# The last wo rows of every layer on 128 partitions, in one transfer over all 16 DMA engines

## The chip, the cores and the metric

The kernel runs on one core of one Trainium2 chip. The metric is the device time of one execution in microseconds (us), here about 1998 us. A single run of the kernel before scatters with a standard deviation of about 1.0 us, one of the changed kernel with about 0.7 us.

## The reference

Four layers of decode attention for one token: A, B, A, B. All arrays are bf16; x has 640 values, there are 32 heads of 192 values, and the caches hold 8192 positions.

```python
x = x + attn(layernorm(x), k_cache, v_cache, wq, wo)      # four times, with the arrays of A, B, A, B

def attn(x, k_cache, v_cache, wq, wo):
    q = (x @ wq).reshape(32 heads, 192)
    p = softmax(q . k_cache * 192 ** -0.5)                # over 8192 positions
    return (p . v_cache).reshape(6144) @ wo               # wo: 6144 x 640
```

Nearly all of the work is reading: the profile counts 848 MB from HBM.

## The kernel before

All loads go through one queue, issued by SyncE. Eight memory slots of 3 MB hold K blocks, V blocks and weights in turn; a transfer is issued when its slot is free. VectorE multiplies K by q in place, TensorE (PE) sums the products, the softmax follows, and PE multiplies by V.

The output projection of a layer is done in four pieces: three blocks of 10 heads (`wo`, 1920 rows each) and a *tail*, `wol`, the 384 rows of the last two heads. The change touches the tail alone. Before, in layers 0 to 2, it lay on 64 partitions with 6 rows each; in layer 3 on 128 partitions with 3 rows each.

```python
O_PART = [P // 2, P // 2, P // 2, P]                      # P = 128
OI = [O_LAST * DH // n for n in O_PART]                   # rows on a partition: 6, 6, 6, 3
# ...
def transfer(n):
    # ...
    if n[0] == "wol":
        r0 = o["wol"] * DH
        if O_PART[l] == P:                                # 128 partitions, one transfer
            return SP.op(lambda s: s.dma_start(
                wol_rows(l), w["wo"][r0:r0 + O_LAST * DH].rearrange("(p i) n -> p (i n)", p=P)),
                *free, sem=semOL, inc=16)
        k = O_PART[l] // O_LAST                           # 64 partitions: one transfer of 32 for each head
        for h in range(O_LAST):
            e = SP.op(lambda s, h=h: s.dma_start(
                wol_rows(l)[h * k:(h + 1) * k],
                w["wo"][r0 + h * DH:r0 + (h + 1) * DH].rearrange("(q e i) n -> e q (i n)", e=8, i=OI[l])),
                *free, sem=semOL, inc=16)
        return e
# ...
def values(h):                                            # the last two heads are written in the tail's order
    # ...
    q = 1 if O_PART[l] == P else O_PART[l] // O_LAST // 8
    parts = [(o_sb[...].rearrange("p (i e q) -> p q e i", i=OI[l], q=q), OB[par][...]) for i in range(2)]
# ...
def gather_last(h):                                       # transposes a head's output: k = OI[l] columns
    n, k = O_PART[l] // O_LAST, OI[l]
    for c in range(k):
        for i in range(2):
            PE.op(lambda t, c=c, i=i: t.matmul(TB[r0:r0 + n, c:c + 1], lhsT=o_sb[...], rhs=pick[:, i:i + 1], ...))
# ...
def project(n, rows, o, ev_o):                            # OI[l] * 5 matmuls for the tail
    for i in range(k):
        for c in range(DC):
            PE.op(lambda t, i=i, c=c: t.matmul(YB[:, c:c + 1], lhsT=t3[:, i, c:D:DC], rhs=o[:, i:i + 1], ...))
```

The source pattern of the old form, `(q e i) n -> e q (i n)` with `e=8`, looks odd.

## Time and profile before

| | before |
|---|---|
| median of the first three runs | 1998.22 us (1997.81 to 1998.73) |
| span of the profiled run | 1996.3 us |
| DMA, main queue, share of 16 engines | 99.3% |
| PE / VectorE busy | 70% / 52% |
| instruction fetches (packets of queue q8) | 71 |

The page of the whole execution. The GB/s line has 40 slices of 50 us; part 3 lists each DMA queue with its packets, megabytes and share of the 16 engines.

```profile
span 1996.3 us, 20649 instructions
PE 1397.3 (70%) x10555; PEld 321.0 (16%) x7611; DVE 1047.7 (52%) x1074; ACT 220.3 (11%) x665; POOL 4.5 (0%) x22
GB/s 412 429 432 428 431 430 429 431 430 430 429 431 429 430 430 430 429 430 430 429 379 430 430 431 428 432 429 430 431 429 426 431 428 431 430 430 430 429 430 335
q1 hardware_dynamic: 40064, 848.38, 99.3%
q8 instruction: 71, 1.16, 0.2%
```

DMA is the bound. The queue runs at about 430 GB/s in all slices but the first, the last and the 21st, the boundary of layers 1 and 2 (379). One packet of 24,576 bytes takes 914 ns in the packet records, 26.9 bytes/ns for one engine.

The boundary of layers 1 and 2, PE's instructions in order of time (start us, duration us, what; in brackets the idle time before and what ended it):

```profile
1017.31 3.16 PE L465 MATMUL YB<-oT,pool 128*128 128x1 bf16 x75 [1.13 <-DMA pool<-in_B_wo_dram]
1020.40 1.35 PE L465 MATMUL YB<-oTl,pool 64*128 64x1 bf16 x30
1022.28 0.59 PE L373 MATMUL TB<-small,ones 128*128 128x2 f32 x2 [0.52 <-DVE small L371]
1023.39 1.78 PE L407 MATMUL QM<-wq,xb 128*128 128x384 bf16 x5 [0.52 <-DVE xb L386]
```

PE waits for the third wo block, projects it (75 matmuls), projects the tail (30 matmuls, 1.35 us), and the next layer starts. The DMA queue runs dry in this stretch (the lowest slice of a window view from 985 to 1050 us is 88 GB/s, just after 1019 us; the spread of a transfer's 16 landings falls from 11.06 us, from 1011.9 us on, to 2.12 us, from 1029.3 us on), so a microsecond here is a microsecond of the kernel.

The end of the chain of waits (start us, duration us, what), and PE's last instructions:

```profile
1932.77 6.77 DVE pool L495 x4
...
1940.07 6.78 DVE pool L495 x4
...
1948.74 43.57 DMA pool<-in_B_wo_dram
1992.32 0.05 issue
1992.36 0.77 PE YB L465 x15
```
```profile
1991.54 0.74 PE L465 MATMUL YB<-oTl,pool 128*128 128x1 bf16 x15
1992.36 0.76 PE L465 MATMUL YB<-oT,pool 128*128 128x1 bf16 x15
```

**Lags of the engines.** In the semaphore records of the trace the transfers of 128 partitions leave 16 landings each, and the six tail transfers of layers 0 to 2 leave 8 each. I take a landing for the end of one engine's share. Sorted, they show how far the engines are apart. An engine keeps its lag from one transfer to the next (the 16 sorted lags at 1406.6 us and at 1413.9 us agree within 0.01 us), so it can be followed. At the third wo block of layer 2 (landed 1507.31 to 1511.72 us) the lags behind the first engine were, in us, H being the half that carries the tail and U the other (which engine belongs to which half shows from the tail's own 16 landings, eight engines twice, 1.15 to 1.17 us apart):

```
H: 0.00 0.00 0.16 0.75 1.81 2.09 3.23 4.21
U: 0.03 0.23 3.06 3.19 3.24 3.25 3.31 4.41
```

Engines fall behind in steps, most of about 1.5 us, just after a 16,384-byte packet of queue q8 (behind the one at 1737.83 us, for example, the largest lag goes from 8.14 to 9.69 us). The profile calls that queue "instruction". There are 71 such packets beside PE's 10,555 matmuls and 7,611 weight loads, one for 255.9 PE instructions. I call such a packet a *fetch*.

### The profile page before, as it was taken

What the parts mean: (1) busy time and instruction counts of PE and PEld (TensorE: products, weight loads), DVE (VectorE), ACT (ScalarE), POOL (GpSimd) and SP (SyncE); (2) the same over time, 40 slices, a digit from 0 to 9 for tenths busy, and PEclk for the clock granted to TensorE, in tenths of its full rate; (3) what the DMA queues carried; (4) which work ended last, traced back from release to release, by engine and by line L of the source; (5) the groups of instructions that cost most, each with busy time, mean ns of one, the idle gap of its engine ahead of it and who ended that gap; (6) DMA issues with size and microseconds to landing.
All of it is one profiled execution on the core that took longest, in us unless ns stands there. A gap on an engine that the chain in (4) does not pass through costs nothing.

```text
span 1996.3 us, 20649 instructions
## 1 busy us (share of the span) xinstructions
PE 1397.3 (70%) x10555; PEld 321.0 (16%) x7611; DVE 1047.7 (52%) x1074; ACT 220.3 (11%) x665; POOL 4.5 (0%) x22
## 2 busy tenths in 40 slices
PE   4667767667576766666777676776776768767776
PEld 1111112111311211211041111121112212111112
DVE  3554554556255456455725545545663455654563
ACT  0111111111011111111011111111101111111111
POOL 0000000000000000000000000000000000000000
PEclk9888877889678788888977878888887788887888
DMA  9999999999999999999999999999999999999997
GB/s 412 429 432 428 431 430 429 431 430 430 429 431 429 430 430 430 429 430 430 429 379 430 430 431 428 432 429 430 431 429 426 431 428 431 430 430 430 429 430 335
DMA packets 40296, 849.69 MB, mean 426 GB/s; under 512 B 4688, under 2 KB 4688, under 8 KB 5136
## 3 DMA queue, kind: packets, MB, share of 16 engines
q1 hardware_dynamic: 40064, 848.38, 99.3%
q8 instruction: 71, 1.16, 0.2%
q14 instruction: 17, 0.14, 0.0%
q10 hardware_dynamic: 144, 0.00, 0.0%
HBM read 848.36 MB, written 0.00 MB: 425 GB/s over the span
## 4 chain that ended last, share of the span: by engine, by line
DMA 69%; PE 18%; DVE 11%; ACT 1%; issue 1%; another core or an unknown queue 0%; SPq 0%; DVEq 0%
DMA pool<-in_B_k_cache_dram 32%; DMA pool<-in_A_k_cache_dram 30%; PE S L58 12%; DVE pool L495 9%; DMA pool<-in_B_wo_dram 4%; PE O L546 2%; DMA pool<-in_A_wo_dram 2%; DMA x_bf<-in_A_x_dram 1%; PE S L508 1%; PE TB L569 1%; PE QT L427 1%; DVE s_sb L516 1%; PE YB L465 1%; ACT p_sb L526 1%; PE TB L530 0%
## 5 line engine op out<-in xcount | busy, mean ns | idle before, releaser
L495 DVE TENSOR_TENSOR pool<-pool,q_sb 128x3072 bf16<-128x3072 bf16 x512 | 865.7, 1754 | 398.8 <-DMA pool<-in_A_k_cache_dram 204.7
L58 PE MATMUL S<-pool,ident 128*128 128x512 bf16 x2944 | 803.4, 427 | 34.6 <-DVE pool L495 34.5
L546 PE MATMUL O<-pool,p_sb 128*2 128x384 bf16 x4096 | 340.1, 414 | 0.0
L508 PE MATMUL S<-pool,ident 128*128 128x512 bf16 x128 | 61.3, 479 | 223.9 <-DVE pool L495 223.9
L516 DVE TENSOR_REDUCE s_sb<-S 128x64 f32<-128x512 f32 x128 | 88.4, 690 | 237.0 <-PE S L58 237.0
L569 PE MATMUL TB<-o_sb,small 128*1 128x192 f32 x480 | 123.9, 391 | 38.1 <-DVE small L534 27.1
L546 PEld LDWEIGHTS O<-pool,p_sb 128*2 128x2 bf16 x4096 | 128.1, 87 | 128.1 <-issue 91.8
L453 ACT ACTIVATE q_sb<-QM 128x192 bf16<-128x192 f32 x120 | 39.6, 330 | 964.1 <-PE QM L446 964.1
L446 PEld LDWEIGHTS QM<-ident,qT 128*128 128x128 bf16 x240 | 23.2, 98 | 745.3 <-issue 729.8
L530 PE MATMUL TB<-small,ones 128*128 128x1 f32 x256 | 50.3, 266 | 109.9 <-ACT p_sb L526 109.9
L520 PE MATMUL QM<-ident,m_bf 128*128 128x128 bf16 x128 | 27.8, 217 | 122.9 <-DVE m_bf L519 121.2
L561 ACT ACTIVATE o_sb<-O,small 128x384 f32<-128x384 f32 (+1 forms) x136 | 77.2, 579 | 224.5 <-PE O L546 224.5
L534 DVE RECIPROCAL small<-TB 128x1 f32<-128x1 f32 x128 | 21.6, 168 | 122.9 <-PE TB L530 122.9
L526 ACT ACTIVATE p_sb<-s_sb,small 128x64 bf16<-128x64 f32 x128 | 44.5, 348 | 268.5 <-DVE small L523 268.5
L523 DVE TENSOR_REDUCE small<-QM 128x1 f32<-128x128 f32 x128 | 37.3, 292 | 63.3 <-PE QM L520 63.3
L575 ACT ACTIVATE orow<-TB 1x192 bf16<-1x192 f32 x120 | 38.3, 319 | 202.7 <-PE TB L569 202.7
L530 PEld LDWEIGHTS TB<-small,ones 128*128 128x128 f32 x256 | 39.5, 194 | 130.4 <-ACT p_sb L526 130.4
L508 PEld LDWEIGHTS S<-pool,ident 128*128 128x128 bf16 x128 | 12.8, 100 | 283.6 <-DVE pool L495 283.3
L520 PEld LDWEIGHTS QM<-ident,m_bf 128*128 128x128 bf16 x128 | 12.3, 96 | 216.7 <-ACT q_sb L453 126.9
L569 PEld LDWEIGHTS TB<-o_sb,small 128*1 128x1 f32 x480 | 33.5, 89 | 81.4 <-DVE small L534 36.0
L465 PE MATMUL YB<-oT,pool 128*128 128x1 bf16 x900 | 38.1, 178 | 6.6 <-DMA pool<-in_A_wo_dram 3.2
L465 PEld LDWEIGHTS YB<-oT,pool 128*128 128x128 bf16 x900 | 37.0, 131 | 7.6 <-DMA pool<-in_A_wo_dram 3.4
(50 smaller groups left out, 220.0 us busy)
## 6 DMA issues: line engine op xcount, KB each, us to landing
pool<-in_B_k_cache_dram SPq DMA_DIRECT2D x64, 3072.0 KB, 35.5
pool<-in_A_k_cache_dram SPq DMA_DIRECT2D x63, 3072.0 KB, 27.7
pool<-in_A_v_cache_dram SPq DMA_DIRECT2D x63, 3072.0 KB, 33.5
pool<-in_B_v_cache_dram SPq DMA_DIRECT2D x60, 3072.0 KB, 37.0
pool<-in_A_wo_dram SPq DMA_DIRECT2D x6, 2400.0 KB, 25.8
pool<-in_B_wo_dram SPq DMA_DIRECT2D x5, 2400.0 KB, 33.9
pool<-in_A_wq_dram SPq DMA_DIRECT2D x1, 7680.0 KB, 20.9
pool<-in_B_wq_dram SPq DMA_DIRECT2D x1, 7680.0 KB, 29.5
```

The source lines that it names most:

```text
L58: return t.add_instruction(mybir.InstMatmult(name=t.bass.get_next_instruction_name(), engine=mybir.EngineType.PE, ins=[t.lower_ap(rhs), t. ...
L453: lambda a: a.activation(q_sb[i][:], QM[:, 0:DH], ACT.Copy), e, last["q"][i], bank=use["QM"])
L465: e = PE.op(lambda t, i=i, c=c, f=y_first[0], fin=end and i == k - 1: t.matmul(YB[:, c:c + 1], lhsT=t3[:, i, c:D:DC], rhs=o[:, i:i + 1], s ...
L495: e = DV.op(lambda v, d0=d0: v.tensor_tensor(k3[:, :, d0:d0 + QD], kin[:, :, d0:d0 + QD], q_sb[qi][:, d0:d0 + QD].unsqueeze(1).broadcast_t ...
L508: t.matmul(S[:, :], lhsT=ident[:], rhs=k3[:, :, d0:d0 + R], start=True, stop=fin) if d0 == 0 else
L516: ev_s = DV.op(lambda v: v.tensor_reduce(s_sb[par][:], S[:].rearrange("p (j r) -> p j r", r=R), AX.X, ALU.add), ev_S[h], last["s"][par], b ...
L520: e = PE.op(lambda t: t.matmul(QM[:, C_MX:C_MX + P], lhsT=m_bf[par][:, 0:1].broadcast_to([P, P]), rhs=ident[:], start=True, stop=True), ev ...
L526: ev_p[h] = AC.op(lambda a: a.activation(p_sb[pi][:], s_sb[par][:], ACT.Exp, bias=negm[par][:, 0:1], accum_out=l_col[par][:]), ev_n, ev_s, ...
L530: e = PE.op(lambda t: t.matmul(TB[:, C_L + par:C_L + par + 1], lhsT=ones[:, 0:1].broadcast_to([P, P]), rhs=l_col[par][:], start=True, stop ...
L546: e = PE.op(lambda e, g=g, j=j, f=m < G, fin=fin: e.matmul(OB[par][32 * g:32 * g + 2, 0:2 * DH], lhsT=p_sb[pi][:, j:j + 2], rhs=t[:, j * D ...
L561: ev_os[h] = AC.op(lambda a, o=o, i=i: a.activation(o, i, ACT.Copy, scale=rl[pi][:, 0:1]), e, ev_rl[h], last["osb"], bank=use[f"O{par}"])
L569: e = PE.op(lambda t, i=i: t.matmul(TB[0:1, C_O:C_O + DH], lhsT=pick[:, i:i + 1], rhs=o_sb[:, i * DH:(i + 1) * DH], start=(i == 0), stop=( ...
```

## The change

The intent is that all 16 engines share the tail of every layer, as they did in layer 3 already (16 landings there). Everything else follows from `O_PART`: one transfer instead of two, 3 rows on a partition instead of 6, 15 projection matmuls instead of 30, and half of the transposes.

```diff
-    O_PART = [P // 2, P // 2, P // 2, P]
+    O_PART = [P] * NL
```

## The prediction

> **What bounds the kernel now.** DMA. The page of the whole execution gives the main queue 99.3% of the 16 engines' span at 425 GB/s; PE is busy 70%, DVE 52%. The chain of waits is 69% DMA. A 24,576-byte packet takes 914 ns: 26.9 B/ns an engine. The slices drop only at the layer 1 to 2 boundary (379 GB/s) and at the end.
>
> **The change.** In layers 0 to 2 the last 384 rows of wo (480 KB) arrive as two transfers of 32 partitions, source dimension 8 outermost. [...] these six transfers leave 9 semaphore updates each (8 landings and one write by the queue), all others 16. So half the engines get 8 packets of 7,680 B (291 ns each, 2.33 us) and the other half nothing. After it every engine gets 8 packets of 3,840 B (149 ns, measured in layer 3, which has this form already): 1.19 us. Bytes stay equal. Also, per layer, 15 fewer projection matmuls (30 take 1.35 us in the timeline, so -0.65 us), 24 fewer transposing matmuls, each with its weight load: 78 PE instructions less, 234 in all.
>
> **What lies on the critical path.** Not the mean of the engines but the last one. From the 16 landing times of each transfer I followed the engines' lags. They grow by about 1.5 us whenever an instruction fetch (16 KB, queue q8, 71 of them) falls on an engine; they reset at the layer 1 to 2 boundary, where the queue runs dry.
> - Layer 0: the latest engine is one of the untouched half (lag 5.0 us, against 3.5 in the half that takes the load). Evening out gains nothing; the untouched half loses 1.19 us.
> - Layer 1 to 2 boundary: the third wo block's last landing (1017.3 us) starts the projection. The loaded half lags 8.8, the other 8.0; with layer 0 evened out they become about 7.6 and 9.2: +0.4 us. The shorter projection then gives -0.65 us, on the chain. Net about -0.2 us.
> - Layer 2: the latest engine is in the loaded half (4.2 before, 6.5 after). It stays latest to the end: lag 11.2 at the last landing (1992.3 us). It gains 1.14 us; the worst of the other half rises from 8.0 to 9.2.
> - The last fetch (at 1989.4 us) falls on that same latest engine and costs 1.5 us. With 234 PE instructions less it should come past the end or not at all; then the other half's 9.2 is the end: -2.0 us instead of -1.1.
>
> Sum: -0.2 and -1.1 to -2.0; I take -1.9.
>
> **Predicted: 1996.3 us, 1994.5 to 1998.8 eight times in ten. Faster by over 2%: 0.003; within 2%: 0.994; slower: 0.003.**
>
> **What would show it.** The queue's packets: 192 of 7,680 B gone, 384 more of 3,840 B. wo's tail transfers with 16 landings within the spread of the engines. The DMA share unchanged at 99%; 70 or 71 fetches; projection of the tail 15 matmuls in 0.7 us; span near 1994.4 us. The last landing near 1990.4.
>
> **What would make it wrong.** Fetches falling on other engines: each costs 1.5 us on one, and the latest one decides. If they fall on the half that now carries more, the gain vanishes or turns into +1 us. A gain of several us would mean that the DMA idled at boundaries where I read none.

The sum: -0.2 us at the boundary and -1.1 to -2.0 at the end, together -1.3 to -2.2, of which -1.9 was taken. That 234 PE instructions are about one fetch is an estimate from the trace of before (255.9 PE instructions to a fetch).

## More of the kernel before

The chain says that the kernel ends 0.8 us after the last DMA landing (1992.32). But PE had been busy with the tail's projection until 1992.28 (1991.54 + 0.74). It waited for the DMA for less than 0.1 us.

## The result, and the profile after

| | before | after |
|---|---|---|
| median, first comparison | 1998.01 us (4 runs) | 1996.58 us (4 runs, 1996.25 to 1997.43) |
| ratio | | 0.9994, 95% interval 0.9977 to 1.0011 |
| span of the profiled run | 1996.3 | 1994.7 |
| last landing before the output | 1992.32 | 1990.08 |
| instruction fetches | 71 | 70 |

A ratio is the mean time of one kernel's fast runs over that of the other's of the same rounds, so it isn't quite the ratio of the medians. The changed kernel was compared three times, on three occasions; the differences of the means were -1.21, -0.89 and -1.49 us. Taken together (14 runs against 22) that is -1.23 us with a standard error of 0.29: a real gain of 0.06%.

The page after:

```profile
span 1994.7 us, 20412 instructions
PE 1392.6 (70%) x10438; PEld 318.0 (16%) x7494; DVE 1047.4 (53%) x1074; ACT 220.3 (11%) x665; POOL 4.5 (0%) x22
GB/s 410 431 431 428 432 429 429 430 431 430 428 430 431 428 432 428 431 429 429 431 382 431 428 431 428 431 430 429 431 429 427 430 430 429 430 429 429 429 432 345
q1 hardware_dynamic: 40256, 848.38, 99.4%
q8 instruction: 70, 1.15, 0.2%
```

The bytes are equal, there are 192 packets more, 117 matmuls and 117 weight loads fewer (234 PE instructions), and one fetch fewer. The boundary of layers 1 and 2:

```profile
1017.86 3.16 PE L465 MATMUL YB<-oT,pool 128*128 128x1 bf16 x75 [0.51 <-DMA pool<-in_B_wo_dram]
1020.88 0.74 PE L465 MATMUL YB<-oTl,pool 128*128 128x1 bf16 x15
1022.14 0.59 PE L373 MATMUL TB<-small,ones 128*128 128x2 f32 x2 [0.52 <-DVE small L371]
1023.25 1.78 PE L407 MATMUL QM<-wq,xb 128*128 128x384 bf16 x5 [0.52 <-DVE xb L386]
```

PE starts on the third wo block 0.55 us *later* (+0.4 predicted), the tail's projection is 0.61 us shorter (-0.65 predicted), and the next layer's q starts 0.14 us earlier (-0.2 predicted). In the two later traces of the changed kernel q starts at 1023.26 and 1023.45, that is 0.13 us earlier and 0.06 us later than before; the sum is thus no larger than its scatter. The end:

```profile
1937.39 1.61 another core or an unknown queue
1939.02 6.77 DVE pool L495 x4
...
1981.81 1.37 another core or an unknown queue
1983.22 2.76 PE O L546 x32
...
1987.86 3.71 PE YB L465 x90
1991.59 0.16 DVE x_bf L633
```
```profile
1990.21 0.74 PE L465 MATMUL YB<-oTl,pool 128*128 128x1 bf16 x15
1990.81 0.74 PE L465 MATMUL YB<-oT,pool 128*128 128x1 bf16 x15
```

"Another core or an unknown queue" is the profile's name for a release that it could not attribute; by the landing records the first was a K block (landed 1939.0), the second the last V block (landed 1983.18). The last landing (1990.08) has left the chain. PE multiplies by the last V block from 1983.22 on, and the final 90 matmuls run without a stop from 1987.86 on; what the end now follows from is that V block and the compute behind it. In the three traces of this kernel the last landing was at 1990.08, 1990.28 and 1990.22, but the span 1994.7, 1996.4 and 1995.3.

### The profile page after: what moved, and what is told of

The parts are those of the page before. It is cut to its first block, busy times and chain, and to the rows that moved or that the text cites. A ratio compares the mean times of both kernels' runs of the same rounds, so it can differ in the third digit from the quotient of the medians.

```text
span 1994.7 us, 20412 instructions
## 1 busy us (share of the span) xinstructions
PE 1392.6 (70%) x10438; PEld 318.0 (16%) x7494; DVE 1047.4 (53%) x1074; ACT 220.3 (11%) x665; POOL 4.5 (0%) x22
## 3 DMA queue, kind: packets, MB, share of 16 engines
q1 hardware_dynamic: 40256, 848.38, 99.4%
## 4 chain that ended last, share of the span: by engine, by line
DMA 65%; PE 21%; DVE 12%; ACT 1%; issue 1%; another core or an unknown queue 0%; DVEq 0%
DMA pool<-in_B_k_cache_dram 32%; DMA pool<-in_A_k_cache_dram 30%; PE S L58 13%; DVE pool L495 10%; PE O L546 3%; DMA pool<-in_B_wo_dram 2%; PE TB L569 1%; DMA x_bf<-in_A_x_dram 1%; PE S L508 1%; PE YB L465 1%; DVE s_sb L516 1%; ACT p_sb L526 1%; PE QT L427 1%; PE TB L530 1%; DVE small L523 0%
## 5 line engine op out<-in xcount | busy, mean ns | idle before, releaser
L546 PE MATMUL O<-pool,p_sb 128*2 128x384 bf16 x4096 | 346.5, 420 | 1.4 <-DMA pool<-in_B_v_cache_dram 1.4
L520 PEld LDWEIGHTS QM<-ident,m_bf 128*128 128x128 bf16 x128 | 12.3, 96 | 215.3 <-ACT q_sb L453 126.9
```

Source lines behind the costliest of these rows:

```text
L520: e = PE.op(lambda t: t.matmul(QM[:, C_MX:C_MX + P], lhsT=m_bf[par][:, 0:1].broadcast_to([P, P]), rhs=ident[:], start=True, stop=True), ev ...
L546: e = PE.op(lambda e, g=g, j=j, f=m < G, fin=fin: e.matmul(OB[par][32 * g:32 * g + 2, 0:2 * DH], lhsT=p_sb[pi][:, j:j + 2], rhs=t[:, j * D ...
```

## The experiments

Twelve runs were made, two of them of the changed kernel as it is. "Before" and "after" are the two kernels above. The theory at the outset: the latest DMA engine counts, not the mean of the 16; fetches and the shorter projection do the rest. Rivals: the balance alone, the instructions alone, or chance.

### The changed kernel again: e0_after_again and g_after_third

No edit. Expected of the first:

> The changed kernel once more, for the size of chance. Theory (the last DMA engine's lag decides): span of the profile within 0.7 us of 1994.7, 70 instruction fetches, landings of the final transfer spread over 7.5 to 9 us, because the fetches fall on the same engines in the same order. Rival (the 1.4 us between the kernels are chance): the span differs by more than 1 us, and the ratio to the kernel before lies on either side of 1.

Measured: 1996.74 us (median of 5), ratio 0.9995 (0.9983 to 1.0008), 70 fetches, last landings spread over 7.95 us. The span of the profiled run was 1996.4, not within 0.7 us of 1994.7: that part of the expectation failed, though the last landing repeated within 0.2 us. By that mark the rival, chance, did better: the spans differ by 1.7 us, though the ratio lies on the same side of 1 as in the first comparison (0.9994). Only the three comparisons together (-1.23 us, standard error 0.29) speak against chance. The end of its chain hangs on a K block (landed 1939.27), and from its multiplication on there is compute alone:

```profile
1939.29 6.78 DVE pool L495 x4
...
1989.17 3.71 PE YB L465 x90
```

This was the first sign that the end is not decided by the last landing.

> The changed kernel a third time, as the base of the two doses on the same chip. Theory: about 1 us under before, 70 fetches; the last landing 1.5 to 2.2 us earlier than in the first trace of before, but the end of the span set by the compute chain of the last heads, not by the last landing.

Measured: 1997.17 us, ratio 0.9992 (0.9979 to 1.0004), 70 fetches, last landing 1990.22 (2.1 us earlier than in the trace of before), span 1995.3. The end of its chain:

```profile
1939.94 47.92 DMA pool<-in_B_wo_dram
1987.86 0.05 issue
1987.91 3.77 PE YB L465 x90
```

It waits for the third wo block (last landing 1987.86), which is followed by the tail and by a last piece of that block; then all 90 matmuls run through, and the last landing at 1990.22 falls within them. The gain, the fetches and the earlier last landing came as expected, and the last landing doesn't set the end. But what sets it here is not the compute chain either: PE waited for a transfer, the third wo block, whose last landing came 2.4 us before the very last. That part of the expectation failed.

### Either half of the change alone: e1_spread_only and e2_short_only

First the balance without the fewer instructions: 64 partitions stay, but in one transfer, meant for 16 engines.

```diff
-                if O_PART[l] == P:
+                if True:
                     return SP.op(lambda s: s.dma_start(
-                        wol_rows(l), w["wo"][r0:r0 + O_LAST * DH].rearrange("(p i) n -> p (i n)", p=P)),
+                        wol_rows(l), w["wo"][r0:r0 + O_LAST * DH].rearrange("(p i) n -> p (i n)", p=O_PART[l])),
@@ values
-                    q = 1 if O_PART[l] == P else O_PART[l] // O_LAST // 8
+                    q = 1
```

> Tail of wo over 16 engines in layers 0 to 2, but still on 64 partitions: 4 packets of 7,680 B on every engine, the same PE instructions as before (71 fetches). Theory: the layer 1 to 2 boundary is not helped (0 to +0.4 us), the latest engine of the end gains 1.16 us and keeps the last fetch: last landing near 1991.4, time 0.7 to 1.1 us under before. Rival 1 (the gain is the shorter projection and fewer instructions): 0. Rival 2 (the gain is the balance alone): the whole 1.4 to 2 us of the change.

Then the fewer instructions without the balance: 128 partitions, in two transfers in the old pattern with `e=8`, which left 8 landings each in before.

```diff
-                if O_PART[l] == P:
+                if l + 1 == NL:
@@ values
-                    q = 1 if O_PART[l] == P else O_PART[l] // O_LAST // 8
+                    q = 1 if l + 1 == NL else O_PART[l] // O_LAST // 8
```

> Tail of wo on 128 partitions (234 PE instructions fewer), but still on 8 engines: 16 packets of 3,840 B (2.38 us)[...]. Theory: the projection at the boundary gives -0.65 us and the last fetch (number 71) goes, which had put 1.54 us on the latest engine: spread of the last landings 9.7 instead of 11.2, time about 2 us under before, so as good as the full change, though the engines are as uneven as before. Rival 1 (shorter projection only, no fetch): -0.65 us with 71 fetches. Rival 2 (balance): 0.

Measured: both kernels were *slower* than either of the whole ones: 2005.91 us (ratio 1.0045, 1.0032 to 1.0057) and 2007.30 us (1.0047, 1.0033 to 1.0061), that is +9.0 and +9.3 us on before in the means of the same rounds. No theory of mine had that. The page of e1_spread_only shows where:

```profile
GB/s 414 428 430 429 431 430 431 428 430 431 405 430 429 430 430 430 429 428 431 430 359 433 429 429 431 431 429 429 431 429 396 429 430 431 430 428 429 431 429 343
```

The 11th, 21st and 31st slices, the ends of layers 0, 1 and 2, lose throughput (405, 359 and 396 against 429, 379 and 426 before). A window view of the end of layer 0 says how (columns: window, length, busy time of each engine, share of PE's full clock that was granted, DMA share, GB/s); before and then e1_spread_only:

```profile
495.00:535.00 40.00, 19.39 (x423) 14.95 (x420) 2.39 (x11) 4.94 (x13) 0.55 (x1) 0.67 1.00 428
```
```profile
495.00:535.00 40.00, 17.28 (x316) 12.05 (x307) 2.39 (x11) 4.61 (x13) 0.55 (x1) 0.67 1.00 398
```

The engines are busy all the time (1.00) in both, but move 398 GB/s instead of 428. So it is not a wait or a gap of the engines: the packets themselves take longer. In the packet records the tail's 7,680-byte packets have a median of 521 ns in e1_spread_only against 292 before; the 3,840-byte packets of e2_short_only 248 against 149 in the changed kernel.

### A new theory: where a transfer writes

What the two slow kernels have in common is another pairing of pattern and partitions:

| form of the tail | partitions written | median packet |
|---|---|---|
| before: two transfers, `e=8` outermost | 0 to 31 and 32 to 63 | 292 ns (7,680 B) |
| after: one transfer | 0 to 127 | 149 ns (3,840 B) |
| e1_spread_only: one transfer, plain order | 0 to 63 | 521 ns (7,680 B) |
| e2_short_only: two transfers, `e=8` outermost | 0 to 63 and 64 to 127 | 248 ns (3,840 B) |

The odd pattern with `e=8` outermost is not idle: into the same 64 partitions, with packets of the same size, two transfers with it took 292 ns a packet and one in the plain order 521. The theory (B; A is still that the latest engine decides): how long a packet takes depends on where its transfer writes. The packet records carry no engine numbers. The runs test the destination alone.

To test the theory without touching the program's own tail, the next kernels move a *dose*: the changed kernel copies the same 384 rows once more into memory that is unused at that moment, at the end of layers 0, 1 and 2. Pattern and partitions of the dose are chosen freely. The results stay right. All doses share this frame (`PE.wait` is in the projection, so that nothing overtakes the dose):

```diff
             if n[0] == "wol":
                 r0 = o["wol"] * DH
+                if l < 3:
+                    i0 = ...                                     # behind the tail, in its own slot
+                    extra[n] = SP.op(lambda s: s.dma_start(<destination>, <source>), *free, sem=semE, inc=16)
@@ project
-                PE.wait(ev_o, need(n), last["YB"])
+                PE.wait(ev_o, need(n), last["YB"], extra.get(n))
```

### The old pattern into partitions 0 to 63 and 64 to 127: f_dose_own and f_dose_other

```diff
+ f_dose_own:   pool[h * 32:h * 32 + 32, i0:i0 + 6 * D]            <- "(q e i) n -> e q (i n)", e=8, i=6, for h in 0, 1
+ f_dose_other: pool[64 + h * 32:64 + h * 32 + 32, i0:i0 + 6 * D]  <- the same
```

> The changed kernel, and in layers 0, 1 and 2 another copy of wo's last 384 rows into unused memory[...] as the kernel before moved it: 32 partitions a transfer[...]. Theory A (the latest engine decides): +2.33 us on half of the engines in each layer, +4 to +5 us in all (layers 0 and 1 meet in one boundary), other packets not slowed: 7,680 B stay at 291 ns. Theory B [...]: the same[...]. Rival (the mean of the engines counts): half of it, +2 to +2.5 us.

> As f_dose_own, same engines, bytes and packet sizes, but into partitions 64 to 127[...]. Theory B [...]: packets of 7,680 B near 500 to 580 ns instead of 291, packets of the other transfers near them slowed too, time +7 to +13 us. Rival (partitions don't matter; something else slowed e1_spread_only and e2_short_only, such as the odd access patterns of o_sb or the form of the source): as f_dose_own, packets at 291 ns.

Measured against before of the same rounds: +3.4 us (2001.84 us median, ratio 1.0017, 1.0004 to 1.0030) and +19.3 us (2018.01, 1.0098, 1.0083 to 1.0114). The changed kernel did not run in these rounds; with its -1.2 us, that is about +4.6 and +20.5 us on it. The first is as expected. The dose's packets had a median of 292 ns in the first and 579 ns in the second. Same source pattern, bytes and packet sizes; only the destination moved by 64 partitions. The windows of the end of layer 0, f_dose_own and f_dose_other:

```profile
495.00:535.00 40.00, 17.91 (x304) 11.81 (x297) 2.38 (x11) 4.94 (x13) 0.55 (x1) 0.67 1.00 426
```
```profile
495.00:535.00 40.00, 15.27 (x263) 9.99 (x251) 1.23 (x10) 4.21 (x11) 0.55 (x1) 0.67 1.01 375
```

Again the share stays at 1.0 and the GB/s fall (375 against 426). The second is more than the 7 to 13 us that I expected: the tail behind the dose suffers too (its 3,840-byte packets had a median of 280 ns, not 149). Not every packet is slowed. In f_dose_other 12 of the 192 dose packets took 291 to 302 ns, the time of an undisturbed one; so a packet to these partitions is not slow in every case. In e1_spread_only 160 of the 192 tail packets took longer than that. What the slow ones waited for, the records do not show.

### The same 64-partition transfer, shifted by 32: g_dose_p0 and g_dose_p32

```diff
+ g_dose_p0:  pool[0:64, i0:i0 + 6 * D]    <- "(p i) n -> p (i n)", p=64        # as e1_spread_only
+ g_dose_p32: pool[32:96, i0:i0 + 6 * D]   <- the same
```

The first was to be slow and the second not.

> The changed kernel and in layers 0 to 2 a further copy of the 384 rows as in e1_spread_only: 16 engines, 4 packets of 7,680 B each, into partitions 0 to 63. [...] Theory [...]: packets of 7,680 B near 450 to 550 ns, others near them slowed too, +8 to +12 us against the changed kernel. Rival (a 64-partition transfer over 16 engines is as good as any): packets at 291 ns, +2.4 to +3.2 us as f_dose_all.

> The same transfer, same engines, same packets, shifted by 32: partitions 32 to 95. [...] Theory [...]: packets at 291 ns, +2.4 to +3.2 us against the changed kernel, as f_dose_all. Rival (64 partitions, or the 7,680 B source runs, are what is slow): as g_dose_p0.

Measured: 2009.14 us (ratio 1.0053, 1.0041 to 1.0066) and 2000.53 us (1.0009, 0.9995 to 1.0023). Against the changed kernel of the same rounds, in the means: +12.3 and +3.3 us; expected were +8 to +12 and +2.4 to +3.2, both a little exceeded. The dose's packets: 516 ns and 292 ns. The windows of the end of layer 0, g_dose_p0 and g_dose_p32:

```profile
495.00:535.00 40.00, 15.26 (x224) 10.38 (x216) 2.38 (x11) 3.35 (x10) 0.55 (x1) 0.61 1.01 405
```
```profile
495.00:535.00 40.00, 18.72 (x345) 12.82 (x338) 2.38 (x11) 4.95 (x13) 0.55 (x1) 0.67 1.00 427
```

This settles that between these two the destination alone decides: 64 partitions in the plain order and 7,680-byte runs are harmless by themselves (292 ns), and 9 us hang on a shift by 32 partitions. The rival of the odd access patterns falls too, because the doses have no compute. The expectations under theory B foretold for all four of these doses which are slow and which not. Why a destination is slow is not shown: no trace names the engines.

### Latest engine or mean engine: f_dose_all

```diff
+ f_dose_all: pool[:, i0:i0 + 3 * D]       <- "(p i) n -> p (i n)", p=128
```

> As f_dose_own, the same bytes over 128 partitions and 16 engines. Theory A: +1.19 us on every engine, +2.4 us in all (layer 1 hidden behind the projection of the third block). Half of f_dose_own, where the rival of the mean expects the same as there.

Measured: 2000.82 us, ratio 1.0012 (0.9999 to 1.0024), +2.3 us on before of the same rounds and so about +3.5 us on the changed kernel, where +2.4 was expected; it is 1.1 us below f_dose_own. With an uncertainty of 0.5 us in that difference, the latest engine (2 to 2.5 us apart) and the mean (0) both miss; the times alone do not decide. The landings do. From the last landing of the third wo block to the last landing of the wq transfer behind the tail, at the end of layer 2:

| | after | f_dose_all | f_dose_own |
|---|---|---|---|
| wo, last landing | 1511.62 | 1512.80 | 1513.41 |
| wq, last landing | 1516.27 | 1518.63 | 1520.32 |
| between them | 4.65 | 5.83 (+1.18) | 6.91 (+2.26) |

A dose of the same bytes delays the latest engine by 1.18 us when 16 engines share it and by 2.26 us when 8 do; 8 packets of 149 and 291 ns are 1.19 and 2.33. The step is right; that the time follows with all of it is not shown.

### Balance and instructions apart, with the destinations kept: e4_padded, f_spread_long and f_half_tail

e4_padded is the changed kernel with idle matmuls at head 20 of layers 0 to 2, and f_spread_long has them exactly where before has its longer tail.

```diff
+            def pad(k):
+                PE.wait(last["QT"], ev_const)
+                for i in range(k):
+                    PE.op(lambda t, i=i: t.matmul(QT[:, 0:1], lhsT=ident[:], rhs=ident[:, 0:1], start=True, stop=True, ...))
@@ e4_padded: layers 0 to 2, head 20
+                    pad(39)
@@ f_spread_long: layers 0 to 2, in gather_last and ahead of the tail's projection
+                    pad(12)
+                    pad(15)
```

> The changed kernel with 39 idle matmuls and their weight loads at head 20 of layers 0, 1 and 2, so that the PE instruction count is that of before (71 fetches). Theory: fetch 71 falls on the engine that in the changed kernel lags 6.6 us and lifts it to 8.1, where two others stand already: no cost, 0 to +0.7 us against the changed kernel. Rival (fewer instructions are the gain): the padding gives back 1.5 us or more.

> The changed kernel with idle matmuls just where before has its longer tail (12 at each of the last two heads, 15 before the tail's projection, in layers 0 to 2): the transfers of after with the PE instructions of before, 71 fetches. Theory: the boundary's projection is 0.65 us longer again, the third fetch of the end costs nothing: +0.3 to +1 us against the changed kernel. Rival (the gain is the balance alone): 0.

Measured: e4_padded 1997.20 us, +0.3 us on the changed kernel of the same rounds, 71 fetches, last landing 1990.42. Giving back the fetch cost nothing that can be seen; the rival's 1.5 us are excluded (the uncertainty is 0.4 us). In its landings the last fetch (at 1987.99) lifts an engine from a lag of 6.4 to 8.1 us, below the latest at 8.4. f_spread_long 1998.39 us, +1.0 us on the changed kernel of the same rounds (uncertainty 0.5 us), 71 fetches, last landing 1990.96. It is at the upper edge of what the theory expected, and two standard errors from nothing. Its trace does not show the reason: the idle matmuls delay the tail's projection by 0.40 us, and q starts at 1023.48, only 0.03 to 0.23 us later than in the three traces of the changed kernel.

f_half_tail is the kernel before with its transfers untouched, but with 3 of the 6 tail columns left out, so its result is wrong:

```diff
 project
-                k = t3.shape[1]
+                k = 3 if n[0] == "wol" else t3.shape[1]
 gather_last
-                for c in range(k):
+                for c in range(3):
```

> The kernel before, transfers untouched, but in layers 0 to 2 only 3 of the 6 tail columns are transposed and projected (a wrong result on purpose): the PE instructions of the changed kernel with the DMA of before, which e2_short_only was meant to be. Theory: 70 fetches, the latest engine spared the last one (-1.5 us) and the boundary's projection shorter (-0.65 us): 1.5 to 2.2 us under before. Rival (balance of the engines alone): 0.

Measured: 1998.55 us (1995.28 to 1998.78), ratio 0.9995 (0.9983 to 1.0008), -0.95 us in the means; 70 fetches. The profiled run happened to be the fastest of the five, with its last landing at 1988.93 and a span of 1993.5, so its trace may not stand for the others. Undecided: less than was expected, and not clearly different from nothing.

So the 1.2 us of the change can't be divided by time. Balance alone gave -0.5 us (f_spread_long) and fewer instructions alone -0.95 us (f_half_tail), uncertain by about 0.5 and 0.7 us.

## Why the prediction was right, and where it was not

- **The time.** Predicted 1996.3 (1994.5 to 1998.8), measured 1996.58, and 1996.74 and 1997.17 in the later rounds. "Within 2%" was right.
- **DMA bounds the kernel, and no bytes are saved.** Right: 99.4% after, the same 848.38 MB.
- **Packets.** Right: 192 packets of 7,680 B are gone, 384 more of 3,840 B at 149 ns are there.
- **The boundary of layers 1 and 2.** Right in both parts: +0.55 - 0.61 against +0.4 - 0.65. The sum, -0.2 predicted, was -0.14, -0.13 and +0.06 us in three traces: right in size, but not clear of scatter.
- **Layer 2's latest engine.** From the last landing of the third wo block to that of the wq transfer behind the tail it took 5.58 us before (1511.72 to 1517.30) and 4.65 us after (1511.62 to 1516.27): -0.93, against -1.14 predicted, and the doses show that the term scales as claimed (1.18 and 2.26 us).
- **The fetches and the last landing.** 70 instead of 71, as foreseen, and the last landing at 1990.1 to 1990.3, close to "near 1990.4". But the last fetch did not "come past the end or not at all": it came at 1986.78 in the trace of after (1988.48 and 1987.81 in the other two). Where its mark is seen it fell on an engine that was not the latest, and so cost nothing: in after it went from a lag of 6.6 to 8.14 us beside one at 8.14, in g_after_third from 6.5 to 8.09 beside one at 8.10. The landing was thus right for a reason that the prediction had only among its risks. In after, where every transfer is shared evenly, the 16 engines drifted apart from 1.7 us behind the boundary of layers 1 and 2 to 8.1 us at the end, 960 us later.
- **The step that was over-sized: that the end follows the last landing one for one ("-2.0 us instead of -1.1").** The fetch itself cost what was said: in the trace of before the lag of the latest engine went from 9.65 to 11.21 us, and the last landing did come 2.0 to 2.2 us earlier. But the time improved by 1.2 us. In before PE had started the final projection at 1989.12, after the third wo block's last landing (1988.41), and its own work ended 0.04 us ahead of the last landing (1992.28 against 1992.32). A last landing that is earlier by more than that meets whatever let PE start. In the three traces of the changed kernel this was another thing each time: the last V block (landed 1983.18), a K block (landed 1939.27) with compute alone behind it, and the third wo block (landed 1987.86). e4_padded can't test this step, because its last fetch fell on an engine that was not the latest. The number held because every term is small beside the stated range of 4.3 us: -1.9 us was predicted and -1.2 measured.
- **What the prediction did not see at all.** It treated an engine's time as its bytes over its own rate. Here that held only for some destinations: 7,680-byte packets had a median of 292 ns in before, f_dose_own and g_dose_p32, but of 516 to 579 ns in e1_spread_only, g_dose_p0 and f_dose_other. Both kernels happen to be on the fast side (292 and 149 ns), so the prediction was not hurt, which was luck; e1_spread_only and e2_short_only, which looked like the harmless halves of the change, were not and lost 9 us.

Still open: how the 1.2 us divide between balance and fewer instructions, and why a dose meant for 16 engines costs 3.3 us (g_dose_p32 against the changed kernel of the same rounds) where its last landing came only 2.5 us later (1992.69 against 1990.22).

## What to carry to other kernels

When DMA is the bound, ask for each transfer how many engines move it (here, its landings) *and which partitions it writes*. A full-share window (1.01) with falling GB/s (405 against 427) and longer packets (516 against 292 ns) was the mark of a bad destination here; moving it by 32 partitions took away 9 us. A landing at the very end is worth only its distance to the next-latest thing: read what the waiting engine was doing just before it, not only that it waited. And to test one half of a change, check first that the half keeps the properties that the whole had by its form.
